# Routing steps go first in a planned instruction list, and gates enter it earlier: attention followed by a sticky mixture of experts on one core

## The chip, the cores and the metric

The kernel runs on one NeuronCore of a Trainium2 chip. The core has a matrix engine (PE, with its weight loads shown as PEld), a vector engine (DVE), an activation engine (ACT), a general engine (POOL) and a queue engine (SP) that here only issues DMAs. Each engine works through its own instructions in order. The metric is device microseconds of one launch, from the first to the last instruction and the little that lies around them.

## The reference

Two stages. First causal attention with a decay, for 8 batches, 8 heads, 576 positions, 64 wide:

```python
scores = scale * np.matmul(q, k.transpose(0, 1, 3, 2))
log_f = np.log(np.clip(f, 0.0001, 1.0))
cum = np.cumsum(log_f, axis=-1)
decay = cum[:, :, :, None] - cum[:, :, None, :]
scores = np.where(causal, -1000000000.0, scores + decay)
attn = softmax(scores)            # max taken off, 1e-9 in the divisor
x = matmul(attn, v)               # (8, 576, 512) after the heads are joined
```

Then each of the 4608 tokens goes through one of 8 experts. The expert is sticky: a token takes the argmax of its own logits where the local gate is below one half (and at position 0), and else the expert of the token before it in its batch.

```python
for b in range(B):
    prev_e = -1
    for s in range(S):
        fresh_e = int(np.argmax(logits[b, s]))
        if s == 0 or local_gate[b, s] < 0.5:
            e = fresh_e
        else:
            e = prev_e if prev_e >= 0 else fresh_e
        prev_e = e
        p = softmax(logits[b, s])
        h = np.maximum(x[b, s] @ w1[e], 0.0)      # 512 -> 1024
        out[b, s] = p[e] * (h @ w2[e])            # 1024 -> 512
```

## The kernel before, in words

**Attention.** Eight batches, one after the other. A batch is cut into 25 units of work (`compute`, from line 836); a unit is a block of 128 queries by up to 512 keys, and passes through stages on different engines: scores on PE (`sc`, L870), row maximum on DVE (`mx`, L881), exponential on ACT (`ex`, L901), transposition of the probabilities on PE (`tr`, L916), their high half on ACT (`hi`, L921), their low half on DVE (`lo`, L925) or, in four units, on PE and ACT (`sub`, `lo2`), products with v on PE (`av`, L895), and the normalisation on DVE (`n1`, `n2`, L956 and L960). Each number in single precision is carried as a high and a low half in 16 bits.

**The list.** Nothing is scheduled at run time. While the program is written, `issue` (L1214) keeps a clock for each engine and, for each stage, the unit that is next in it. It estimates when each could start (`start_of`, L1144), adds that stage's weight `W`, and writes out the instruction whose sum is least; `RANK` decides ties. The costs are constants in the code. Limited buffers (PSUM banks `psS`, `psT`, `psX`, and others) are counted in `room`. `step` (L1253) puts a unit into the lists and issues until that unit's scores are out, so "step 14" of a batch means the place in the list where unit 14 enters.

**What else goes into the list.** While batch b is computed, the next batch's q, k and v are split into halves on POOL, through `queue`, from which `pump` (L310) writes out a share at each step. q and k are then transposed on PE in five groups each (`tq`, L451) and moved out of PSUM by ACT (L460) or DVE (L462, L464) (`eq`). From which step on each group may enter is in `TS`; which engine takes it out (A for ACT, D for DVE) is in `TE`. A finished batch's x is split on POOL (`xr`, and `xl` for its last 64 rows), transposed by DMAs of the SP queue (L756, L785) and written to `xs` in DRAM.

**Gate and routing.** These are the side steps: a chain of small functions, `chain`, of which only the first can go. At step `GI[...]` of batch b, the gate of batch b-1 is put at the front of the chain: `mult` on PE (L819), `half` on ACT, `add` on DVE. In batches 2, 4 and 6 the routing of the two batches before it (a group: 0, 1, 2) is put behind it (`route`, L1333): argmax, the sticky scan, each token's place within its expert, and the inversion of that by matmuls (L1485, L1535). It begins with `mxs` (L1346) and ends with `pinvert2` (L1539). Groups 0 and 1 do part of it on POOL; group 2 does all of that on DVE. Behind group 2 stand `early_idx` and `early_tok`: the indices and the gather (L1628) of 384 tokens of expert 0, which the experts' first matmuls need. `early_tok` may go only once batch 7 has passed step 5, when memory is freed for it. A function that has `yield` in it is several pieces, each with the cost that it yields; `POOL` there means 1500 ns on POOL.

What is left of the chain when attention's lists are empty is written out in order (L1753):

```python
    while chain:
        side_issue(*side_next())
```

**Experts.** Then come the experts (`experts`, L1633): z = x w1 (L1660), relu on ACT (L1646) with its low half on DVE (L1647), y = h w2 (L1674), scaled by ACT (L1651) and scattered by POOL (L1652). Expert 0's first 384 tokens go first; the gate of batch 7 and the last routing group (3) are woven into them.

In what follows a stretch of the trace between attention's last product (L895) and the experts' first (L1660) is called the hole.

Of the kernel before, what the change touches and what calls it, by code (L numbers as in the profile page):

```python
# [38 lines left out]
ORDA = moves_of("q0:P k:M 0:V 1:V k:ag")  # L39
ORDB = moves_of("q:ag q0:T 2:V q1:P k0:P k1:P q:e k:e 3:V q1:T q:Tl k0:T :vl :Vl q:2 q:C 0:K k1:T :iv v0:P k:2 1:K")  # L40

GI = (21, 20, 20)
LI = (14, 18)
PX = 6
XI = 3

TS = {"q": (10, 14, 14, 17, 18), "k": (18, 20, 21, 21, 21)}
TE = {"q": "DDADD", "k": "DDDDA"}

UO = tuple(range(25))  # L50
NP = 0
# [15 lines left out]
def kernel(  # L67
# [13 lines left out]
    B, H, S, D = q.shape  # L81
# [660 lines left out]
        clock["DVE"] += 600  # L742


    XT = {}

    def finish_main(b, xn):
        xr = pools["small"].tile([128, 4, 2, DM], F16, name="xr", bufs=1)
        xt = pools["small"].tile([128, 4, 8, 128], F16, name="xt", bufs=1)
        XT[b] = [xt]  # L750
        xm = xn.rearrange("p (c h) x -> p c (h x)", c=4)
        t0 = b * S
        todo = []

        def turn_x(c):
            nc.sync.dma_start_transpose(out=xt[:, c:c + 2].rearrange("p c a x -> p (c a) x"),  # L756
                                        in_=xr[:, c:c + 2].rearrange("p c a e -> p (c a e)"))
            R[c] = True

        def put_x(r):  # L760
            nc.sync.dma_start(out=xs[t0:t0 + 512].rearrange("(c p r) e -> r p c e", c=4, r=2)[r],
                              in_=xr[r * 64:(r + 1) * 64].rearrange("p c a e -> p c (a e)"))

        R = {}
        bulk.extend([(0 if b == B - 1 else PX + 2 * r, lambda: 2 in R, lambda r=r: put_x(r)) for r in range(2)])
        if b == B - 1:
            def part(c, n, fast, turn):
                split(xr[:, c:c + n, 0, :], xr[:, c:c + n, 1, :], xm[:, c:c + n], fast)
                if turn:
                    turn_x(turn - 1)  # L770

            return [lambda: part(0, 2, False, 1), lambda: part(2, 1, False, 0), lambda: part(3, 1, True, 3)]
        for c in range(0, 4, 2):
            todo += hi_lo(xr[:, c:c + 2, 0, :], xr[:, c:c + 2, 1, :], xm[:, c:c + 2], 1)
            todo.append((0, lambda c=c: turn_x(c)))
        queue.extendleft(reversed(todo))

    def finish_last(b, xnl):
# [5 lines left out]
        def turn_x():  # L784
            nc.sync.dma_start_transpose(out=xlt, in_=xl.rearrange("p a j d -> p (a j d)"))  # L785
            put_xl()

        def put_xl():
            for r in range(2):
# [11 lines left out]
    def gate(b):  # L801
# [29 lines left out]

        if b == B - 1:
            return [lambda: mult((0, 1)), lambda: mult((2, 3, 4)), half, add]
        return [mult, half, add]

    def compute(b, T):
# [293 lines left out]
    STAGES = ("sc", "mx", "mn", "ex", "tr", "hi", "lo", "sub", "lo2", "av", "n1", "n2", "tq", "eq")  # L1130
    RANK = {st: 0.0 for st in STAGES + ("side",)}
    RANK["side"] = -20
    RANK.update({'sc': -20.2, 'mx': 39.7, 'mn': -7.5, 'ex': 80.9, 'tr': -11.9, 'hi': -3.6, 'lo': 1.1, 'sub': 15.5, 'lo2': 1.2, 'av': 12.4, 'n1': -23.3, 'n2': -3.6, 'side': -52.7, 'tq': 30.8, 'eq': -17.3})
    W = {st: 0 for st in RANK}
    W.update({'sc': -100, 'mx': -220, 'mn': -450, 'ex': 40, 'tr': -160, 'hi': -90, 'lo': -350, 'sub': -140, 'lo2': -70, 'av': -70, 'n1': -250, 'n2': -290, 'side': -180, 'tq': -170, 'eq': -430})
    clock = {"PE": T0, "ACT": T0, "DVE": T0, "POOL": T0}
    due = deque()
    pools = {}
# [5 lines left out]
    def start_of(st):  # L1144
# [17 lines left out]
        for r, c in takes.items():  # L1162
            if len(room[r]) < c:
# [4 lines left out]

    COSTS = {"mult": ("PE", 1100), "half": ("ACT", 116), "add": ("DVE", 200), "rows": ("PE", 200), "rows2": ("ACT", 260),
             "ends": ("PE", 30), "carries": ("PE", 30), "back": ("PE", 60), "place": ("PE", 90), "marks": ("DVE", 485),  # L1170
             "prob2": ("ACT", 150), "pmarks": ("DVE", 1500 if B < 2 else 0), "invert": ("PE", 400), "pinvert": ("PE", 600),
             "nop": ("PE", 0), "fill": ("PE", 30)}
    POOL = 1
    OPENS = "mult", "rows", "ends", "carries", "back", "place", "invert", "pinvert", "fill"
    SHUTS = "add", "rows2", "hold", "scan1", "onehot", "place2", "invert2", "pinvert2", "fill2"
    chain = deque()
# [7 lines left out]
    def side_next():  # L1184
        eng, cost = COSTS.get(chain[0].__name__, ("DVE", 160))
        after = [side["end"]]
        if chain[0] is early_tok and "open" not in EX:
            return None, eng, cost
        if chain[0].__name__ in OPENS and side["run"] is None:
            if not room["psS"]:  # L1190
                return None, eng, cost
            after.append(min(room["psS"]))
        return max([clock[eng]] + [t + WAIT[src, eng] for t, src in after]), eng, side["cost"] or cost

    def side_issue(t, eng, cost):
        fn = chain[0]
# [17 lines left out]
    def issue(until=None):  # L1214
        while any(line.values()):
            ready = [(start_of(st), line[st][0][0] + RANK[st], st) for st in STAGES if line[st]]
            if chain:
                ready.append((side_next()[0], serial[0] + RANK["side"], "side"))
            t, _, st = min((x for x in ready if x[0] is not None), key=lambda x: (x[0] + W[x[2]], x[1]))
            if due and due[0][0] <= t and all(room[r] for r in due[0][2]):  # L1220
                due.popleft()[1]()
# [111 lines left out]
    def route(g, last):  # L1333
# [6 lines left out]
        NV = nc.vector  # L1340
# [122 lines left out]
        def marks():  # L1463
# [2 lines left out]
            LO = R["LO"] = rtile([128, GC, 128], F16, "LO")  # L1466
            NV.tensor_tensor(HI, imain.unsqueeze(1).broadcast_to([128, GC, NM]),
                              R["hm"].unsqueeze(2).broadcast_to([128, GC, NM]), ALU.is_equal)
            yield 1400
            if big is NV:  # L1470
                NV.tensor_scalar(RH[:, :, 0], HI, irow[:, 0:1], None, ALU.mult)
                yield 200
                NV.tensor_scalar(RH[:, 4::5, 0], HI[:, 4::5], irow[:, 1:2], None, ALU.mult)
                yield 1900
            else:
                big.tensor_scalar(RH[:, :, 0], HI, irow[:, 0:1], 1.0, ALU.mult, ALU.mult)
                big.tensor_scalar(RH[:, 4::5, 0], HI[:, 4::5], irow[:, 1:2], 1.0, ALU.mult, ALU.mult)
# [48 lines left out]
        def pmarks():  # L1526
            rp = R["rp"] = rtile([128, GC, 3, NM], F16, "rp")
            for j in range(3):
                big.tensor_tensor(rp[:, :, j], R["HI"], pp[:, gs, j].unsqueeze(2).broadcast_to([128, GC, NM]),
                                  ALU.mult)  # L1530

# [170 lines left out]
    EX = {}  # L1702
# [340 lines left out]
```

## Time and profile before

| | us |
|---|---|
| median of 3 runs | 953.27 (949.66 to 957.69) |
| profiled execution | 954.87 |
| its span | 953.2 |
| PE busy in the span | 813.7 (85%) |
| DVE busy | 545.8 (57%) |
| ACT busy | 403.5 (42%) |
| POOL busy | 416.9 (44%) |
| mean granted TensorE clock | 0.939 |

The page gives the busy time of each engine, strips of 40 equal slices in tenths, the chain of work that ended last, and groups of instructions by line. Answers of the trace give the same by stage, and the instructions in order of time: start in us from the span's start, length, engine, line, operation, written from read, count, and in brackets the idle time before and what ended it. An instruction marked SPq or POOLq is one of an engine's queue. Columns of the other views are named where they are shown.

### The profile page before, as it was taken

What the parts mean: (1) busy time and instruction counts of PE and PEld (TensorE: products, weight loads), DVE (VectorE), ACT (ScalarE), POOL (GpSimd) and SP (SyncE); (2) the same over time, 40 slices, a digit from 0 to 9 for tenths busy, and PEclk for the clock granted to TensorE, in tenths of its full rate; (3) what the DMA queues carried; (4) which work ended last, traced back from release to release, by engine and by line L of the source; (5) the groups of instructions that cost most, each with busy time, mean ns of one, the idle gap of its engine ahead of it and who ended that gap; (6) DMA issues with size and microseconds to landing.
All of it is one profiled execution on the core that took longest, in us unless ns stands there. A gap on an engine that the chain in (4) does not pass through costs nothing. (4 is left out here: it accounts for less than half of the span.)

```text
span 953.2 us, 21059 instructions
## 1 busy us (share of the span) xinstructions
PE 813.7 (85%) x8558; PEld 557.8 (59%) x8558; DVE 545.8 (57%) x1135; ACT 403.5 (42%) x769; POOL 416.9 (44%) x479
## 2 busy tenths in 40 slices
PE   4887989999999999711486997799999999999993
PEld 2665878788787878501243663464747465655651
DVE  8775888989988988635272585531425242432200
ACT  4864767777777778500031321221222323131110
POOL 9585975667594946772112304303030212223020
PEclk9888999999999999955698999799999999999997
DMA  6879877697876726150237629927283836423010
GB/s 162 185 149 212 203 153 173 123 209 117 206 146 159 125 58 179 57 138 1 66 117 191 190 89 221 283 58 210 94 231 104 210 128 166 144 78 96 1 41 6
DMA packets 210244, 130.58 MB, mean 137 GB/s; under 512 B 149054, under 2 KB 185024, under 8 KB 210060
## 3 DMA queue, kind: packets, MB, share of 16 engines
q1 hardware_dynamic: 202369, 104.83, 48.3%
q0 software_dynamic: 7776, 24.39, 7.9%
q8 instruction: 68, 1.11, 0.5%
q14 instruction: 31, 0.25, 0.1%
HBM read 77.39 MB, written 20.41 MB: 103 GB/s over the span
## 5 line engine op out<-in xcount | busy, mean ns | idle before, releaser
L1660 PE MATMUL z<-xT,wh 128*128 128x320 f16 (+3 forms) x1088 | 195.2, 299 | 27.8 <-DVE hl L1647 16.4
L901 ACT ACTIVATE P<-st,nm 128x512 f32<-128x512 f32 (+3 forms) x288 | 150.3, 588 | 35.1 <-DVE nm L881 26.1
L1660 PEld LDWEIGHTS <-wh 128*128 128x128 f16 x1088 | 106.2, 99 | 71.6 <-issue 29.5
L881 DVE TENSOR_REDUCE nm<-st 128x1 f32<-128x512 f32 (+4 forms) x264 | 133.1, 542 | 20.2 <-PE st L877 14.3
L1628 POOL DMA_INDIRECT xg<-xs,mg x37 | 44.8, 1212 | 218.5 <-DMA xT<-xg 177.3
L921 ACT CAST ph<-pt 128x512 f16<-128x512 f32 (+1 forms) x200 | 114.1, 584 | 52.2 <-PE pt L916 46.0
L1674 PE MATMUL y<-uh,hh 128*128 128x512 f16 x328 | 125.0, 381 | 7.1 <-ACT o L1651 7.1
L916 PE MATMUL pt<-ident,P 128*128 128x128 f32 x784 | 121.3, 283 | 10.4 <-DVE pl L925 5.8
L925 DVE TENSOR_TENSOR pl<-pt,ph 128x512 f16<-128x512 f32 x168 | 111.0, 674 | 28.6 <-ACT ph L921 20.5
L1646 ACT ACTIVATE hh<-z 128x640 f16<-128x640 f32 (+3 forms) x80 | 48.5, 607 | 184.1 <-PE z L1660 171.2
L1674 PE MATMUL y<-ul,hh 128*128 128x512 f16 x328 | 124.9, 381 | 0.0
L1674 PE MATMUL y<-uh,hl 128*128 128x512 f16 x328 | 124.8, 381 | 0.0
L1660 PE MATMUL z<-xT,wl 128*128 128x320 f16 (+3 forms) x544 | 124.4, 299 | 0.0
L1647 DVE SCALAR_TENSOR_TENSOR hl<-z,hh 128x640 f16<-128x640 f32 (+3 forms) x80 | 55.8, 701 | 114.3 <-ACT hh L1646 114.3
L1674 PEld LDWEIGHTS <-hh 128*128 128x128 f16 x656 | 64.2, 98 | 82.6 <-issue 8.5
L916 PEld LDWEIGHTS pt<-ident,P 128*128 128x128 f32 x784 | 84.7, 143 | 24.3 <-DVE pl L925 7.8
L895 PE MATMUL xp<-VH,ph 128*128 128x65 f16 (+1 forms) x960 | 90.3, 197 | 0.0
L895 PE MATMUL xp<-VL,ph 128*128 128x65 f16 (+1 forms) x960 | 89.1, 195 | 0.0
L895 PE MATMUL xp<-VH,pl 128*128 128x65 f16 (+1 forms) x960 | 88.5, 194 | 0.2
L870 PE MATMUL st<-KB,QB 70*128 70x256 f16 (+4 forms) x448 | 79.5, 288 | 9.8 <-DMA KB<-Ak 6.4
L1652 POOL DMA_INDIRECT out_dram<-o,ms x37 | 39.9, 1077 | 107.8 <-ACT o L1651 66.4
L895 PEld LDWEIGHTS <-ph 128*128 128x128 f16 (+1 forms) x1920 | 80.9, 102 | 9.1 <-issue 5.3
(346 smaller groups left out, 1286.5 us busy)
## 6 DMA issues: line engine op xcount, KB each, us to landing
stg<-in_moe_w_dram SPq DMA_DIRECT2D x64, 512.0 KB
xs<-xr SPq DMA_DIRECT2D x16, 512.0 KB
ldq<-in_q_dram SPq DMA_DIRECT2D x14, 512.0 KB
ldk<-in_k_dram SPq DMA_DIRECT2D x14, 512.0 KB
ldv<-in_v_dram SPq DMA_DIRECT2D x28, 256.0 KB
KB<-Ak SPq DMA_DIRECT2D x14, 256.0 KB
QB<-Aq SPq DMA_DIRECT2D x13, 256.0 KB
ldv<-in_v_dram SPq DMA_DIRECT2D x20, 64.0 KB
```

The source lines that it names most:

```text
L870: nc.tensor.matmul(st[p0:p0 + m, co:co + n], lhsT=queries(lq, kk, h, c), rhs=rhs, start=(ps == 0 and first and co == col), stop=(ps == 1), ...
L881: nc.vector.tensor_reduce(dst, src, axis=AX.X, op=ALU.max, negate=True)
L895: nc.tensor.matmul(xo, lhsT=a[:, c0:c0 + m], rhs=w[:, vi, :], start=False, stop=(i == n - 1 and jj == 2), skip_group_check=True)
L901: nc.scalar.activation(P[:, c0:c1].rearrange("p (k x r) -> p k r x", r=2, x=64), st[:, c0:c1].rearrange("p (k r x) -> p k r x", r=2, x=64) ...
L916: nc.tensor.matmul(U["pt"][:, i * 128:(i + 1) * 128], lhsT=P[:, i * 128:(i + 1) * 128], rhs=ident, is_transpose=True, start=(i == 0), stop ...
L921: nc.scalar.copy(U["ph"][:, :cols], U["pt"][:, :cols])
L925: nc.vector.tensor_tensor(U["pl"][:, :cols], U["pt"][:, :cols], U["ph"][:, :cols], ALU.subtract)
L1628: nc.gpsimd.indirect_dma_start(out=xg, out_offset=None, in_=xs[0:rows], in_offset=bass.IndirectOffsetOnAxis(ap=cols(i), axis=0))
L1646: nc.scalar.activation(hv, z[:, 0:nh, 0:wd], AF.Relu)
L1647: nc.vector.scalar_tensor_tensor(lv, z[:, 0:nh, 0:wd], 0.0, hv, ALU.max, ALU.subtract)
L1660: nc.tensor.matmul(z[:, a, 0:wd], lhsT=w[:, d, fc * 128:(fc + 1) * 128], rhs=xT[:, x, a * wd:(a + 1) * wd], start=(i == 0), stop=(i == len ...
L1674: nc.tensor.matmul(y, lhsT=a[:, fc, t * 128:(t + 1) * 128], rhs=u[:, fc], start=(i == 0), stop=(i == len(prods) - 1))
```

## The change

Numbers and a few lines of the list's writer. `GI`: in batches 2 to 5 the gate enters at step 14, in batches 6 and 7 at step 12, each at 20 before; batch 1 keeps 21. The side steps had one constant weight, -180; now it is set anew before each choice by `side_weight`: -700 if the piece is one of POOL's or can start no later than its engine is free, and 0 if the engine would have to idle for it. The start of a POOL piece is no longer taken from DVE's clock. A gate (but that of batch 7) may go only when all three transposes of its batch's x have been issued, which `XD` counts; until then nothing of the chain goes. The pieces of `marks` and `pmarks` are given other costs, and `pmarks` is cut into pieces. All weights and ranks of the other stages are set anew, and so are `TS` and `TE`: q's groups become ready at later steps, and of the ten groups of a batch ACT takes five instead of two.

```diff
-GI = (21, 20, 20)
+GI = (21, 14, 12)
+
+SW = (-700, 0, 0)
...
-TS = {"q": (10, 14, 14, 17, 18), "k": (18, 20, 21, 21, 21)}
-TE = {"q": "DDADD", "k": "DDDDA"}
+TS = {"q": (13, 17, 18, 19, 20), "k": (19, 20, 20, 21, 21)}
+TE = {"q": "ADDDA", "k": "DAAAD"}
...
-    XT = {}
+    XT, XD = {}, {}
...
             R[c] = True
+            XD[b] = XD.get(b, 0) + 1
...
             put_xl()
+            XD[b] = XD.get(b, 0) + 1
...
+        mult.batch = b
         return [mult, half, add]
...
-    W.update({'sc': -100, 'mx': -220, 'mn': -450, 'ex': 40, 'tr': -160, 'hi': -90, 'lo': -350, 'sub': -140, 'lo2': -70, 'av': -70, 'n1': -250, 'n2': -290, 'side': -180, 'tq': -170, 'eq': -430})
+    W.update({'sc': -210, 'mx': -60, 'mn': -710, 'ex': -30, 'tr': -180, 'hi': -210, 'lo': -140, 'sub': -410, 'lo2': -360, 'av': -130, 'n1': -200,
+              'n2': -170, 'tq': -210, 'eq': -50})
...
-             "prob2": ("ACT", 150), "pmarks": ("DVE", 1500 if B < 2 else 0), "invert": ("PE", 400), "pinvert": ("PE", 600),
+             "prob2": ("ACT", 150), "pmarks": ("DVE", 0), "invert": ("PE", 400), "pinvert": ("PE", 600),
...
-        if chain[0] is early_tok and "open" not in EX:
+        if chain[0] is early_tok and "open" not in EX or XD.get(getattr(chain[0], "batch", None), 0) < 3 and hasattr(chain[0], "batch"):
             return None, eng, cost
...
-        return max([clock[eng]] + [t + WAIT[src, eng] for t, src in after]), eng, side["cost"] or cost
+        now = 0 if side["cost"] is POOL else clock[eng]
+        return max([now] + [t + WAIT[src, eng] for t, src in after]), eng, side["cost"] or cost
+
+    def side_weight(t, eng, cost):
+
+        if t is None:
+            return 0
+        return SW[0] if cost is POOL or t <= clock[eng] + SW[2] else SW[1]
...
                 ready.append((side_next()[0], serial[0] + RANK["side"], "side"))
+                W["side"] = side_weight(*side_next())
...
             for j in range(3):
+                yield 570 if big is NV else POOL
                 big.tensor_tensor(rp[:, :, j], R["HI"], pp[:, gs, j].unsqueeze(2).broadcast_to([128, GC, NM]),
                                   ALU.mult)
```

More of the change, by code (lines that the diff above doesn't have):

```diff
@@ L1132 @@
     RANK["side"] = -20
-    RANK.update({'sc': -20.2, 'mx': 39.7, 'mn': -7.5, 'ex': 80.9, 'tr': -11.9, 'hi': -3.6, 'lo': 1.1, 'sub': 15.5, 'lo2': 1.2, 'av': 12.4, 'n1': -23.3, 'n2': -3.6, 'side': -52.7, 'tq': 30.8, 'eq': -17.3})
+    RANK.update({'sc': 24.3, 'mx': 16.8, 'mn': -67.5, 'ex': 93.3, 'tr': -65.0, 'hi': 26.5, 'lo': -10.3, 'sub': 17.2, 'lo2': 31.3, 'av': 16.7, 'n1': 33.1,
+                 'n2': 10.6, 'side': -52.7, 'tq': 28.8, 'eq': -19.5})
     W = {st: 0 for st in RANK}
-    W.update({'sc': -100, 'mx': -220, 'mn': -450, 'ex': 40, 'tr': -160, 'hi': -90, 'lo': -350, 'sub': -140, 'lo2': -70, 'av': -70, 'n1': -250, 'n2': -290, 'side': -180, 'tq': -170, 'eq': -430})
+    W.update({'sc': -210, 'mx': -60, 'mn': -710, 'ex': -30, 'tr': -180, 'hi': -210, 'lo': -140, 'sub': -410, 'lo2': -360, 'av': -130, 'n1': -200,
+              'n2': -170, 'tq': -210, 'eq': -50})
     clock = {"PE": T0, "ACT": T0, "DVE": T0, "POOL": T0}
@@ L1468, in marks @@
                               R["hm"].unsqueeze(2).broadcast_to([128, GC, NM]), ALU.is_equal)
-            yield 1400
+            yield 320 if big is NV else 1480
             if big is NV:
                 NV.tensor_scalar(RH[:, :, 0], HI, irow[:, 0:1], None, ALU.mult)
-                yield 200
+                yield 250
                 NV.tensor_scalar(RH[:, 4::5, 0], HI[:, 4::5], irow[:, 1:2], None, ALU.mult)
-                yield 1900
+                yield 2060
             else:
```

## The prediction

> **What bounds the kernel now.** I read the utilisation strips of the page first, then the table of busy time by stage, then the order of instructions of PE and of DVE around the hole that the strips show. The strips (40 slices of 23.8 us):
>
> ```profile
> PE   4887989999999999711486997799999999999993
> POOL 9585975667594946772112304303030212223020
> ```
>
> PE is nine tenths busy in attention and again in the experts, and falls to one tenth for two slices between them. The table by stage (stretch, length, then busy time of PE, PEld, DVE, ACT, POOL with counts, granted clock, DMA share, GB/s):
>
> ```profile
> 100.00:406.30 306.30, 290.55 (x4855) 238.24 (x4851) 266.58 (x603) 230.00 (x487) 213.57 (x245) 0.99 0.68 146
> 406.30:438.40 32.10, 3.53 (x30) 2.21 (x28) 10.53 (x33) 1.04 (x3) 24.35 (x34) 0.55 0.39 102
> 438.40:455.90 17.50, 3.87 (x31) 2.31 (x31) 13.14 (x55) 0.63 (x2) 0.00 (x0) 0.50 0.01 1
> 455.90:467.00 11.10, 0.01 (x1) 0.04 (x2) 1.15 (x10) 0.00 (x0) 3.13 (x3) 0.50 0.62 142
> ```
>
> Attention is bound by PE (290.6 of 306.3 us, clock 0.99), with DVE next (266.6). Then come three stretches, 60.7 us together, in which PE does 7.4 us. What fills them is in the order of instructions (start, length, engine, line; first PE's, then DVE's, then POOL's):
>
> ```profile
> 406.05 0.20 PE L895 MATMUL xp<-VH,pl 128*64 128x65 f16 x2
> 426.10 0.22 PE L1442 MATMUL st<-EX,ones 128*128 128x80 f16 x1 [10.04 <-POOL EX L1435]
> 466.99 0.80 PE L1660 MATMUL z<-xT,wh 128*128 128x384 f16 x2 [11.24 <-DMA xT<-xg]
> ```
> ```profile
> 166.25 0.24 DVE L1346 TENSOR_REDUCE mx<-L 128x10 f32<-128x80 f32 x1
> 398.45 0.28 DVE L1539 TENSOR_TENSOR invp<-st,invp 128x120 f32<-128x120 f32 x1 [1.64 <-PE st L1535]
> 398.64 0.23 DVE L1346 TENSOR_REDUCE mx<-L 128x10 f32<-128x80 f32 x1
> 438.58 0.23 DVE L1346 TENSOR_REDUCE mx<-L 128x10 f32<-128x80 f32 x1
> 455.69 0.28 DVE L1539 TENSOR_TENSOR invp<-st,invp 128x120 f32<-128x120 f32 x1 [1.09 <-PE st L1535]
> ```
> ```profile
> 423.09 2.26 POOL L308 TENSOR_TENSOR ul<-stg,uh 128x512 f16<-128x512 f32 x2
> 456.79 1.23 POOL L1628 DMA_INDIRECT xg<-xs,xg  x1 [19.66 <-DVE xe L1569]
> ```
>
> L1346 opens a routing group, the L1539 before the next one closes it. Group 0 runs 166 to 398, spread over five batches. Groups 1 and 2 run after attention with nothing beside them: 40 us and 17 us. Only then can the gather of the early expert's tokens start (456.8) and the first expert matmul (467.0). So the hole is routing that the list pushed out of attention.
>
> **The change, part by part.** *Routing first (weight -700 where the engine need not idle), gates at step 14 or 12.* The question is whether groups 0 to 2 now fit into attention. Step 20's diagonal masks date the steps:
>
> ```profile
> L976 PE MATMUL st<-mB,mA x4: 193/193/202, 341.4 to 341.5; 128*128 128x64 f16 x4
> L976 PE MATMUL st<-mB,mA x4: 193/193/202, 384.8 to 384.9; 128*128 128x64 f16 x4
> ```
>
> A batch is 43.4 us, a step 1.74 us. Group 2 joins the chain at step 12 of batch 6, 8 steps before 341.4: at 327.5. The two costliest DVE groups of attention (busy, mean ns, idle before):
>
> ```profile
> L881 DVE TENSOR_REDUCE nm<-st 128x1 f32<-128x512 f32 (+4 forms) x218 | 109.8, 544 | 5.6 <-PE st L877 3.5 <-PE st L870 1.0
> L925 DVE TENSOR_TENSOR pl<-pt,ph 128x512 f16<-128x512 f32 (+1 forms) x139 | 91.7, 673 | 20.6 <-ACT ph L921 13.9 <-PE xp L895 3.5 <-ACT P L992 1.7
> ```
>
> After a routing piece on DVE the next is not ready at once, so one attention operation (about 0.6 us) goes between, then the piece (about 0.2): 0.8 us a piece. By the code, group 2 has some 52 DVE pieces (42 us), 4 us in its large marks, and some 19 crossings between engines, estimated at 0.6 us: about 57 us. It has 327.5 to 406, 78 us, less the time that the chain stands behind a gate (some 5 us in each of batches 6 and 7) and two gates of 2 us: 64 us. It just fits. Groups 0 and 1, with 17 POOL pieces counted at 1.5 us and four empty steps, come to about 70 us and have two batches each. I take it that all three fit and that the gather (10.2 us from 456.8 to 467.0) lies beside the end of attention, leaving 2 us exposed. Gain: the 60.7 us less what attention grows by.
>
> *What attention grows by.* (a) PE takes in the routing matmuls of groups 1 and 2: 3.5 + 3.9 us at half clock, above; **6 us** (4 to 7.4), as PE has nothing to spare. (b) DVE takes in 10.5 + 13.1 us, about 21 without attention's own tail, and small operations are longer there (min/median/max):
>
> ```profile
> L1397 DVE TENSOR_TENSOR_SCAN crow<-hold,ends x4: 169/626/1115, 223.4 to 483.4; 1x10 f16<-1x10 f32 x4
> L1467 DVE TENSOR_TENSOR HI<-imain,hm x4: 574/576/1339, 317.3 to 491.9; 128x400 f16<-128x400 f16 x4
> L1359 DVE TENSOR_REDUCE F<-eq x4: 227/236/237, 192.4 to 478.1; 128x10 f32<-128x80 f32 x4
> ```
>
> Two-input L1397 and L1467 cost 0.9 and 0.8 us more at 223 and 317, with POOL busy, than alone; the reduction does not. I allow 6 us more for each group. The Trainium skill's page "GPSIMD Engine Reference", section "Key points", says that GpSimd shares its SBUF interfaces with VectorE and collides with DVE instructions that have two SBUF inputs or run in a two-port mode; it speaks against this change, as it puts group 2 beside a working POOL, and the rows agree. By that rule alone DVE would take in 33 us, without it 21.
>
> *Evictions of q's and k's groups.* Three full groups a batch move from DVE to ACT:
>
> ```profile
> L464 DVE COPY Ak<-st x24: 680/692/693, 119.1 to 344.8; 128x1024 f16<-128x1024 f16 x24
> L460 ACT ACTIVATE Aq<-st x6: 1024/1025/1025, 99.1 to 326.5; 128x1024 f16<-128x1024 f16 x6
> ```
>
> Over six batches DVE loses 18 x 0.69 = 12.4 us and ACT gains 18 x 1.02 = 18.4 us, which its 76 idle us cover (306.3 - 230.0). If that cover failed, it would cost at most the 6 us of difference. DVE's net gain in work is 9 to 21 us against 40 idle; the part in batches 6 and 7 comes thick, so **5 us** on the path (-5 to 12). The later steps for q's groups crowd the transposes into steps 17 to 20; I put them, the new ranks and the other weights at nothing (-5 to 8), since PE's own work is unchanged.
>
> (c) *Waits for POOL.* The plan counts 1.5 us for a POOL piece from the end of the one before; in its queue it stands behind all that was pumped. Rows for hand-overs in group 0:
>
> ```profile
> 309.20 1.00 DVE L1459 SCALAR_TENSOR_TENSOR ov<-code,ov 128x10 f32<-128x10 f32 x1
> 340.70 0.23 DVE L1504 TENSOR_REDUCE den<-ex 128x10 f32<-128x80 f32 x1
> ```
> ```profile
> 314.62 0.21 POOL L1461 TENSOR_TENSOR hm<-t,ov 128x10 f16<-128x10 f32 x1
> 341.07 0.40 POOL L1506 TENSOR_TENSOR ex<-ex,OHA 128x80 f32<-128x80 f32 x1 [2.59 <-DVE den L1504]
> ```
>
> One was 4.4 us late, the other 0.1. Before, the slow chain hid it; now the next DVE or PE piece of the routing is queued right behind, and with it all attention work of that engine. Groups 0 and 1 have four such hand-overs each (L1357, L1435, L1461, L1506). The plan covers 1.5 us of it; with one in four 4.4 - 1.5 = 2.9 us late, 8 x 0.25 x 2.9 is **6 us** (0 to 8 x 4.4 = 35).
>
> (d) *Gates ahead of their data.* The guard holds the gate until its three transposes are issued, not until they land. Batch 7:
>
> ```profile
> 371.05 1.05 POOL L1604 TENSOR_SCALAR stg<-stg 128x1024 f32<-128x1024 f32 x1 [7.25 <-DMA stg<-in_moe_w_dram]
> 384.21 0.41 POOL L304 TENSOR_SCALAR xl<-xnl 128x256 f16<-128x256 f32 x1
> 385.40 1.23 SPq L785 DMA_TRANSPOSE xlt<-xl  x1
> 386.04 0.95 PE L819 MATMUL st<-wg,xt 128*128 128x18 f16 x32
> 387.89 0.42 PE L819 MATMUL st<-wg,xlt 128*64 128x18 f16 x8 [0.90 <-DMA xlt<-xl]
> ```
>
> At step 20 PE already waits 0.9 us for xlt. POOL makes xl behind 13 us of weight pieces that start when the first staged block lands (371.1); the list has them by about step 15 (estimated from 17 steps for 24 pieces), so the guard opens there, 5 steps or 8.7 us of PE's time earlier, while POOL gets there no sooner. PE is in order: all of attention stands behind this gate. I take 6 us here and 2 in batches 5 and 6 together: **8 us** (0 to 14).
>
> *The experts' start.* The first 14 matmuls of z against 14 later ones, in the chain of waits:
>
> ```profile
> 466.99 4.45 PE z L1660 x14
> 479.19 2.45 PE z L1660 x14
> 495.59 1.31 PE y L1674 x6
> ```
>
> Without the hole they run at full clock: 2 us saved. The Trainium skill's page "TensorE: Matmul & The Clock Gate", section "Part 1", says that an idle window of about 3.4 us halves the clock. The rows agree for the long hole; by that rule a 6 us stand at (d) would cost some 2 us more, and the sum would be 920. Next to be late would be y, which needs the last weights: POOL ends them at 425.4, 19 us after attention's end, and y comes 28.6 us after z's start. That covers it.
>
> **Sum.** Attention grows by 6 + 5 + 6 + 8 = 25 us and ends at 431.3; z starts at 433.3. Saved: 467.0 - 433.3 + 2 = 35.7. The profiled execution took 954.87 (span 953.2 and 1.7 around it), 1.6 above the median 953.27: 919.2 on its own scale, 918 on the median's.
>
> **Rivals.**
> - *No stall* (chance 0.18): (b), (c) and (d) hide in DVE's 40 and PE's 16 idle us. For it: ACT's slack and 12.4 us off DVE. z at 406.3 + 6 + 2 = 414.3, saved 54.7: about 899.
> - *Routing doesn't get through* (0.20): chain pieces take 1.1 us instead of 0.8, or the gate of batch 6 holds the chain longer, and much of group 2 runs behind attention. For it: only 7 us are spare above. Up to 17.1 + 11.3 us (438.6 to 455.7 to 467.0) stay exposed: attention +16, z at 450.9, saved 16 us: about 938; with the gather alone exposed, 928.
> - *POOL's backlog decides* (0.06, slower): if each of the eight hand-overs of (c) waits 10 us, all of it lands on DVE and PE: 80 us against 41.7 of gain (35.7 + 6), about 992. It decides from 41.7 / 8 = 5.2 us a hand-over. Against it: the longest here is 4.4.
> - *The list shifts the holes about* (0.04): what is saved comes back as bubbles in attention, within 1%.
>
> The forecast itself gets 0.52. The range from 896 to 942 reaches from the no-stall case to the routing rival. A measurement of this kernel can tell about 1% from no change. Faster by over 1% (below 943.7): 0.87; within 1%: 0.07; slower: 0.06.
>
> **What would show it.** Right: L1539 three times before attention's last L895; the gather (L1628) issued before it; z within some 5 us of it; PE's strip without the slices of one tenth; L895 ending near 431. PE waiting at L819 for xlt in batch 7 shows (d), DVE or PE waiting for POOL at L1359, L1442, L1467 or L1510 shows (c). Wrong: an L1346 after the last L895, or attention ending beyond 445.

## Result and the profile after

The changed kernel takes 921.78 us, the median of four runs (920.49 to 926.55). The kernel before took 954.7 us beside it (949.66 to 957.69). The ratio is 0.967, with an interval of 0.961 to 0.973. The profiled execution of the changed kernel took 921.67 us; its span is 919.9 and its granted clock 0.964, where the one before had 953.2 and 0.939.

The first view is again the page's strips of the changed kernel, PE and its clock, in 40 slices, now of 23.0 us.

```profile
PE   5787999889997998688896997899999999999993
PEclk9888999999999999889998998999999999999997
```

The two slices of one tenth are gone. In their place PE's strip has some slices of six to eight tenths inside attention, which stood at nine before. In this version lines 895, 1660, 1628, 1539 and 1346 of before are 900, 1676, 1644, 1555 and 1361. Attention's last product and the experts' first one, from the lists of each line's instructions (min/median/max in ns, first and last start):

```profile
L900 PE MATMUL xp<-VH,pl x960: 190/193/247, 26.0 to 437.0; 128*128 128x65 f16 x128, 128*64 128x65 f16 x64
L1676 PE MATMUL z<-xT,wh x1088: 216/299/421, 437.1 to 898.5; 128*128 128x320 f16 x149, 128*128 128x384 f16 x11, 128*128 128x256 f16 x11, 128*128 128x128 f16 x11
```

Before, these times were 406.1 and 467.0. Attention ends 31 us later, and the experts follow it at once. The order of DVE's and of POOL's instructions shows the three groups and the gather:

```profile
227.30 0.27 DVE L1555 TENSOR_TENSOR invp<-st,invp 128x120 f32<-128x120 f32 x1
253.60 0.22 DVE L1361 TENSOR_REDUCE mx<-L 128x10 f32<-128x80 f32 x1
328.70 0.27 DVE L1555 TENSOR_TENSOR invp<-st,invp 128x120 f32<-128x120 f32 x1
355.27 0.22 DVE L1361 TENSOR_REDUCE mx<-L 128x10 f32<-128x80 f32 x1
414.10 0.28 DVE L1555 TENSOR_TENSOR invp<-st,invp 128x120 f32<-128x120 f32 x1 [0.51 <-PE st L1551]
```
```profile
418.25 1.23 POOL L1644 DMA_INDIRECT xg<-xs,xg  x1 [1.87 <-DVE rs L961]
```

Group 2 is closed at 414.1, and the gather starts at 418.3, 19 us before attention's end.

Where did the 31 us of attention come from? The table by stage, cut at step 20 of batches 1 to 7, at the last product, and with the same columns as the table by stage in the prediction (stretch, length, busy time of PE, PEld, DVE, ACT, POOL with counts, granted clock, DMA share, GB/s). The three stretches shown are the ones that grew, with the sum of all seven. First the kernel before, then the changed kernel.

```profile
162.70:204.30 41.60, 40.76 (x686) 33.95 (x682) 37.63 (x89) 32.83 (x71) 28.31 (x27) 1.00 0.74 151
250.50:293.10 42.60, 41.52 (x710) 34.81 (x704) 38.58 (x90) 33.68 (x73) 33.68 (x35) 1.00 0.77 161
341.40:384.80 43.40, 41.70 (x680) 33.39 (x677) 35.90 (x86) 33.40 (x72) 24.16 (x30) 1.00 0.46 125
sum 292.40, PE 276.67 PEld 226.71 DVE 253.69 ACT 217.85 POOL 200.17; mean PE 39.52 PEld 32.39 DVE 36.24 ACT 31.12 POOL 28.60
```
```profile
157.70:212.00 54.30, 47.69 (x762) 38.48 (x755) 46.44 (x111) 38.42 (x80) 39.94 (x51) 0.97 0.69 151
259.30:313.40 54.10, 46.55 (x761) 37.55 (x754) 45.63 (x110) 38.43 (x80) 39.67 (x50) 1.00 0.65 132
361.10:417.50 56.40, 47.05 (x715) 37.34 (x713) 51.72 (x127) 36.33 (x76) 29.42 (x27) 0.91 0.44 110
sum 325.20, PE 291.32 PEld 236.39 DVE 272.71 ACT 237.25 POOL 216.78; mean PE 41.62 PEld 33.77 DVE 38.96 ACT 33.89 POOL 30.97
```

The stretches shown hold most of a routing group each: group 0 in 157.7 to 212.0, group 1 in 259.3 to 313.4, group 2 in 361.1 to 417.5. They grew by 12.7, 11.5 and 13.0 us. The four stretches left out changed by -3.1, 1.1, -0.6 and -1.8. By the two sum rows the seven stretches grew by 32.8 us, of which PE is busy for 14.6 more (291.3 against 276.7) and idle for 18.2 more (33.9 against 15.7). The grown stretches show that the price is paid where the routing runs, not after it.

PE's waits in the changed kernel, from 112.0 to 437.2 (us in total, times, longest):

```profile
PE pt L921 <- DVE pl L930: 8.3, 11, 1.7
PE st L875 <- ACT P L906: 7.4, 8, 4.6
PE st L823 <- DMA xlt<-xl: 3.7, 2, 2.3
PE xp L900 <- DVE pl L930: 3.5, 4, 1.3
PE pt L921 <- DVE rs L961: 3.0, 4, 1.5
PE st L875 <- DMA KB<-Ak: 1.7, 1, 1.7
PE xp L890 <- DVE xn L965: 1.6, 2, 1.0
```

And in the kernel before, from 113.9 to 406.3:

```profile
PE pt L916 <- DVE pl L925: 5.1, 9, 1.2
PE xp L885 <- DVE xn L960: 2.7, 5, 1.1
PE pt L916 <- ACT P L901: 2.0, 3, 0.9
PE st L1535 <- POOL rp L1529: 1.8, 1, 1.8
PE st L819 <- DMA xlt<-xl: 0.9, 1, 0.9
```

After, 23.8 us of the rows shown are waits for DVE, or for an ACT exponential, which in its turn often waits for DVE's maximum (25.9 us of ACT's time in this stretch of the trace); before, those were 9.8. With the rows under 1 us, which are left out here, it is 25.7 against 11.6: 14.1 us of the 18.2 by which PE is longer idle. The longest of these waits is worth seeing in full, since it shows how group 2's marks are placed. DVE's order in batch 7 of the changed kernel, where ... leaves out two marks:

```profile
380.59 0.65 DVE L1476 TENSOR_TENSOR hm<-t,ov 128x10 f16<-128x10 f32 x1
381.27 1.37 DVE L1482 TENSOR_TENSOR HI<-imain,hm 128x400 f16<-128x400 f16 x1
382.68 1.10 DVE L1486 TENSOR_SCALAR RH<-HI,irow 128x400 f16<-128x400 f16 x1
...
385.23 1.48 DVE L1494 TENSOR_TENSOR LO<-i,lo 128x1280 f16<-128x1280 f16 x1
386.64 0.68 DVE L886 TENSOR_REDUCE nm<-st 128x1 f32<-128x512 f32 x1
```

Six pieces of routing stand in a row, 6.0 us from 380.6 to 386.6, and the maximum that attention waits for comes behind them. The exponential that it releases starts on ACT at 387.35, after ACT had waited 7.0 us for DVE. The next two views are matmuls in PE's order with the waits before them, and PE by stretches of five microseconds (stretch, length, PE's busy time, clock, DMA share, GB/s). PE stands 4.6 us, and the clock is halved in the stretch in which it starts again. A second, shorter loss of clock follows from 401:

```profile
388.11 0.59 PE L875 MATMUL st<-Ak,Aq 128*128 128x512 f16 x1 [4.59 <-ACT P L906]
400.01 0.66 PE L921 MATMUL pt<-ident,P 128*128 128x128 f32 x4 [0.99 <-DVE pl L930]
402.48 1.06 PE L921 MATMUL pt<-ident,P 128*128 128x128 f32 x4 [0.89 <-DVE rs L961]
```
```profile
386.00:391.00 5.00, 2.89 (x11) 0.50 1.09 205
401.00:406.00 5.00, 3.98 (x51) 0.66 0.46 150
```

The Trainium skill's page "TensorE: Matmul & The Clock Gate", section "Part 1", says that one idle window of about 3.4 us brings the half clock. The wait of 4.6 us agrees with that; the trace as a whole does not, as shorter waits were followed by the half clock too. By stretches of one microsecond the clock is 0.50 from 403 to 405, behind waits of 0.99 and 0.89 us, and from 188 to 190, behind one of 1.74 us; in the 4.6 us wait itself, which begins at 383.5, it is 0.73 from 385 to 386 and 0.50 from 386 on. A wait of 1.26 us before 173.1 left it at 1.00. So here some waits of one to two microseconds cost clock and others did not.

### The profile page after: what moved, and what is told of

Read it like the earlier page. It is cut to its first block, busy times and chain, and to the rows that moved or that the text cites. A ratio compares the mean times of both kernels' runs of the same rounds, so it can differ in the third digit from the quotient of the medians.

```text
span 919.9 us, 21034 instructions
## 1 busy us (share of the span) xinstructions
PE 816.4 (89%) x8558; PEld 559.8 (61%) x8558; DVE 538.4 (59%) x1117; ACT 420.4 (46%) x787; POOL 420.9 (46%) x479
## 4 chain that ended last, share of the span: by engine, by line
PE 59%; POOL 13%; DVE 9%; DMA 8%; issue 5%; ACT 3%; SPq 1%; POOLq 0%; ACTq 0%; DVEq 0%
PE z L1676 21%; PE y L1690 18%; PE pt L921 6%; PE st L875 6%; PE xp L900 4%; POOL t16q L310 2%; DMA stg<-in_moe_w_dram 2%; POOL xr L310 2%; DMA out_dram<-o,xs 2%; POOL t16k L310 2%; DMA KB<-Ak 2%; DVE pl L930 1%; ACT P L906 1%; PE st L453 1%; DVE nm L886 1%
## 5 line engine op out<-in xcount | busy, mean ns | idle before, releaser
L1676 PE MATMUL z<-xT,wh 128*128 128x320 f16 (+3 forms) x1088 | 191.6, 296 | 15.4 <-DVE hl L1663 15.2
L906 ACT ACTIVATE P<-st,nm 128x512 f32<-128x512 f32 (+3 forms) x288 | 152.7, 585 | 38.3 <-DVE nm L886 35.4
L926 ACT CAST ph<-pt 128x512 f16<-128x512 f32 (+1 forms) x200 | 116.0, 583 | 62.8 <-PE pt L921 61.5
L921 PE MATMUL pt<-ident,P 128*128 128x128 f32 x784 | 125.6, 284 | 16.8 <-DVE pl L930 9.6
L1644 POOL DMA_INDIRECT xg<-xs,mg x37 | 46.7, 1262 | 188.7 <-DMA xT<-xg 168.3
L900 PE MATMUL xp<-VH,pl 128*128 128x65 f16 (+1 forms) x960 | 92.1, 195 | 4.6 <-DVE pl L930 4.6
L900 PE MATMUL xp<-VH,ph 128*128 128x65 f16 (+1 forms) x960 | 94.1, 198 | 0.9 <-ACT ph L926 0.9
L900 PE MATMUL xp<-VL,ph 128*128 128x65 f16 (+1 forms) x960 | 92.9, 196 | 0.0
L900 PEld LDWEIGHTS <-ph 128*128 128x128 f16 (+1 forms) x1920 | 84.7, 103 | 8.6 <-issue 3.3
```

The lines of the kernel that those rows point to most:

```text
L900: nc.tensor.matmul(xo, lhsT=a[:, c0:c0 + m], rhs=w[:, vi, :], start=False, stop=(i == n - 1 and jj == 2), skip_group_check=True)
L906: nc.scalar.activation(P[:, c0:c1].rearrange("p (k x r) -> p k r x", r=2, x=64), st[:, c0:c1].rearrange("p (k r x) -> p k r x", r=2, x=64) ...
L921: nc.tensor.matmul(U["pt"][:, i * 128:(i + 1) * 128], lhsT=P[:, i * 128:(i + 1) * 128], rhs=ident, is_transpose=True, start=(i == 0), stop ...
L926: nc.scalar.copy(U["ph"][:, :cols], U["pt"][:, :cols])
L1676: nc.tensor.matmul(z[:, a, 0:wd], lhsT=w[:, d, fc * 128:(fc + 1) * 128], rhs=xT[:, x, a * wd:(a + 1) * wd], start=(i == 0), stop=(i == len ...
```

## Experiments

All ratios are against the kernel before, timed on the same chip, with their 95% intervals. The changed kernel itself has 0.967. "Ends" is the start of the last product of attention in the experiment's profile, "z" that of the experts' first matmul; the changed kernel has 437.0 and 437.1.

**The old weights, ranks and evictions, with everything else of the change.**

```diff
-TS = {"q": (13, 17, 18, 19, 20), "k": (19, 20, 20, 21, 21)}
-TE = {"q": "ADDDA", "k": "DAAAD"}
+TS = {"q": (10, 14, 14, 17, 18), "k": (18, 20, 21, 21, 21)}
+TE = {"q": "DDADD", "k": "DDDDA"}
...
(RANK and W of the stages: the numbers of before)
```

> The side steps' new weight, the guard, the early gates and the new piece costs alone; weights and ranks of the other stages and the steps and engines of q's and k's groups as before. Theory A (routing itself makes attention longer, by DVE, PE and POOL work and waits): the hole is gone and attention grows about as in the changed kernel or a little more, since DVE keeps 12.4 us of evictions; 920 to 932. Rival B (the new weights and the crowded transposes make it longer): hole gone without the growth, 895 to 908.

Measured: 936.7 us, ratio 0.980 (0.976 to 0.983). Attention ends at 443.6, z starts at 443.8. The rule for the side steps, with the early gates and the pieces' costs, closes the hole without the new numbers of the stages, at a price of 37.5 us in attention (443.6 against 406.1). The new numbers take 6.6 us off that, and by the ratios some 12 us off the whole time (0.980 against 0.967); 4.9 us of it lie behind z's start (487.7 us of span here, 482.8 in the changed kernel). The time lies above the range that was expected; I had those numbers at nothing.

**The new weights alone: old gates, old constant weight of the side steps.** The pieces' costs, the count of transposes and the start of POOL pieces stay as changed, here and in the other kernels with the old constant weight.

```diff
-GI = (21, 14, 12)
+GI = (21, 20, 20)
-SW = (-700, 0, 0)
+SW = (-180, -180, 0)
```

> The new weights, ranks, steps and engines alone; the side steps keep the constant -180 and the gates step 20. Theory A: the hole stays, attention as before or slightly shorter: 945 to 956. Rival B: the hole stays and attention is 25 to 31 us longer: 975 to 985.

Measured: 945.85 us, ratio 0.987 (0.983 to 0.990). Attention ends at 408.6, z starts at 460.4: the hole is still there, 52 us long. That the new numbers lengthen attention is thereby refuted: it ends only 2.5 us later than before, although it now has most of group 1 beside it, which begins at 327 and is closed at 432, where before it ran from 398.6 to 438.4. The gains of these two kernels, 1.3% and 2.0%, add up to the 3.3% of the whole change.

**The gates back at step 20.**

```diff
-GI = (21, 14, 12)
+GI = (21, 20, 20)
```

> The changed kernel with the gates at step 20 again. In its list group 2 ends nine DVE instructions before attention does, so the gather of the early tokens no longer lies beside attention. Theory A: 5 to 10 us of the gather come out behind attention, 925 to 932. Rival D (early gates cost more by PE waiting for xlt than they bring): some 4 us of waits go, 914 to 920.

Measured: 928.66 us, ratio 0.970 (0.967 to 0.973). Attention ends at 424.9, 12 us sooner than with the early gates, and z starts at 435.1: the gather lies bare, as expected. The order of POOL's instructions in this kernel:

```profile
423.55 1.22 POOL L1644 DMA_INDIRECT xg<-xs,xg  x1 [0.52 <-DVE xe L1585]
```

The shorter attention was not expected. The two stretches in which groups 0 and 1 begin take 48.7 us each here, 54.3 and 54.1 in the changed kernel. So early gates are needed for group 2 and cost something in the batches of groups 0 and 1.

**The old constant weight, with the early gates.**

```diff
-SW = (-700, 0, 0)
+SW = (-180, -180, 0)
```

> The changed kernel with the constant weight -180 for the side steps, gates at 14 and 12 kept. Theory A: group 0 takes as long as before, most of group 1's end and all of group 2 run behind attention, and the hole is back at 35 to 60 us: 940 to 956. Rival E (the early gates alone bring the routing through): 918 to 930.

Measured: 934.27 us, ratio 0.976 (0.974 to 0.979). Attention ends at 411.0 and z starts at 446.2. Groups 0 and 1 get through (closed at 281.2 and 401.3), group 2 runs from 402.1 to 435.0, most of it behind attention. The time lies between the two ranges expected. With the kernel of old gates (hole 52 us), this shows what each part does: the early gates by themselves bring two groups into attention and shorten the hole from 52 to 35 us; the weight of -700 brings in the third. By the kernel with the gates at 20 it does so without early gates too, only too late for the gather.

**The small pieces of groups 0 and 1 on DVE, so that nothing waits for POOL at a hand-over.**

```diff
-        aux, AUX = (nc.gpsimd, POOL) if big is nc.gpsimd else (NV, None)
+        aux, AUX = NV, None
```

> The changed kernel, with the small POOL pieces of groups 0 and 1 (eq, EX, cnt, lo, hm, ex, pp, pe) on DVE instead; the large marks stay on POOL. Theory C (DVE and PE waiting for POOL at the hand-overs is what makes attention longer): those waits go, attention 5 to 10 us shorter, ratio to the kernel before 0.957 to 0.963. Theory F (DVE's own time, with routing pieces ahead of attention's low halves and maxima, is what makes it longer): 14 more pieces a group on DVE, attention 5 to 12 us longer, ratio 0.972 to 0.980.

Measured: 929.88 us, ratio 0.970 (0.964 to 0.977). The groups themselves are shorter, 60 and 62.6 us instead of 73.9 and 75.1, but attention ends at 439.7, 2.7 us later. The ratio lies between the two ranges expected. The edit takes away the hand-overs to POOL (term c) and puts 14 more pieces of each group on DVE, so it shows the sum of both: at most a small gain from the first, or one that the second took back. That the first is small is seen in the changed kernel, where DVE waits 2.4 us for POOL in all of attention and PE not at all.

**Group 2's large pieces on POOL as well.**

```diff
-        big = nc.vector if g >= B // 2 - 2 else nc.gpsimd
+        big = nc.vector if g >= B // 2 - 1 else nc.gpsimd
```

> The changed kernel, with group 2 done as groups 0 and 1 are: its small pieces and large marks on POOL. In its list group 2 ends with attention, so the gather of 10 us comes out behind it. Theory F: batch 7 gets some 8 us shorter by DVE's relief, which the gather takes back: ratio 0.965 to 0.973. Theory C: POOL in batch 7 is full of weight pieces, DVE and PE wait behind them at four hand-overs, some 5 us each: ratio 0.985 to 0.998.

Measured: 953.89 us, ratio 0.998 (0.996 to 1.000): the whole gain is gone. This edit brings about what the rival with POOL's backlog says. DVE's and PE's longest waits in this kernel from 361.2 to 437.4, and the stage behind attention:

```profile
DVE pe L1525 <- POOL ex L1521: 10.3, 1, 10.3
PE pt L921 <- DVE rs L961: 9.7, 1, 9.7
```
```profile
437.40:465.80 28.40, 0.37 (x18) 0.27 (x13) 4.80 (x13) 0.40 (x1) 16.80 (x16) 0.59 0.71 163
```

One hand-over made DVE wait 10.3 us and, through it, PE 9.7. The group is closed at 437.2, 0.2 us before the last product. The steps between it and the gather (4.1 us in the changed kernel, 414.1 to 418.3) fall behind attention, and there the list has POOL's weight pieces (13.6 of the 16.8 us of POOL in that stage; the rest is the gather itself) ahead of the gather, which starts at 455.6. z comes at 465.8. Two things thus turn the result: a hand-over behind POOL's queue, and a group that is closed too late for the gather to be written before attention's end.

**The pieces of groups 0 and 1 back at -180, group 2 as changed.**

```diff
+        if getattr(chain[0], "g", 2) in SLOW or chain[0] is nop:
+            return SLOW_W
         return SW[0] if cost is POOL or t <= clock[eng] + SW[2] else SW[1]
...
+SLOW, SLOW_W = (0, 1), -180
```

> The changed kernel, with the pieces of groups 0 and 1 at the weight -180 again; group 2, the gates and the early tokens keep -700. In its list group 1 ends just ahead of group 2's start, and group 2 ends with attention (672 of 670 DVE instructions), so the gather of 10 us is exposed. Theory F with the price on density (a group that goes through in one batch costs some 12 us, one that is spread costs little): attention 10 to 20 us shorter, 10 us given back: ratio 0.955 to 0.967. If a group costs the same however fast it goes: 0.975 to 0.980.

Measured: 941.79 us, ratio 0.985 (0.981 to 0.990). Step 20 of batch 7 comes at 402.9 instead of 417.5, though some of this is work of group 2 that now stands later. Group 2 starts at 370.6, is closed at 433.9, and the last product is at 432.2. The same cliff shows in POOL's order of this kernel:

```profile
439.35 1.04 POOL L1626 TENSOR_SCALAR stg<-stg 128x1024 f32<-128x1024 f32 x1 [7.88 <-DMA stg<-in_moe_w_dram]
...
448.65 1.23 POOL L1650 DMA_INDIRECT xg<-xs,xg  x1 [0.18 <-issue]
```

The gather stands behind weight pieces for 14.7 us after the group was closed, and z starts at 458.8. For part of that POOL itself stands, until a block of weights lands at 439.35. The ratio lies above both ranges expected: the exposed end cost more than the 10 us that I had allowed, and what a slower passage of groups 0 and 1 is worth is seen here only in part.

**The pieces go first even where their engine has to idle for them**, at a weight of -350 instead of -700.

```diff
-SW = (-700, 0, 0)
+SW = (-350, -350, 0)
```

> The changed kernel with -350 for every side piece, also where its engine would idle for it. In its list group 2 ends 90 DVE instructions before attention does instead of 43. If idling for a routing piece costs what it looks like (some 0.1 to 0.2 us on DVE or PE for each of some 180 pieces): attention 10 to 25 us longer, nothing gained at its end, ratio 0.977 to 0.993. Rival: those gaps lie in slack, and a routing that is through sooner changes nothing: 0.964 to 0.970.

Measured: 942.35 us, ratio 0.984 (0.979 to 0.989). Group 2 takes 27.4 us (351.6 to 379.0) instead of 58.8, the gather starts at 406.1, and attention ends at 449.7, 12.7 us later. PE's waits in this kernel's attention:

```profile
PE xp L900 <- DVE pl L930: 12.2, 6, 3.8
PE st L823 <- DMA xlt<-xl: 11.9, 2, 8.1
```

A chain that is through earlier gains nothing, and a gate ahead of its data does cost what term (d) feared: 8.1 us at one gate. In the changed kernel the longest such wait is 2.3 us. Its rule, "only where the engine need not idle", is the likely reason; the run does not show it alone, since the weight itself changed too.

**Early gates for group 2 alone.**

```diff
-GI = (21, 14, 12)
+GI = (21, 20, 12)
```

> The changed kernel with the gates at step 20 in batches 2 to 5 and at 12 only in batches 6 and 7, so that groups 0 and 1 start after their batch's transposes and group 2 still starts early; in its list group 2 ends 45 DVE instructions before attention does. Theory G (what groups 0 and 1 cost depends on where they fall: started at step 14 they meet the crowd of transposes and evictions of steps 17 to 21): batches 3 and 5 take some 49 us, as in the run with all gates at 20, instead of 54, attention ends some 10 us sooner than in the changed kernel and z follows at once: ratio to the kernel before 0.953 to 0.960. If a group costs the same wherever it starts: the changed kernel's ratio, 0.964 to 0.970.

Measured: 919.22 us, ratio 0.961 (0.958 to 0.965), just above the range expected. Attention ends at 424.2, 12.8 us sooner than in the changed kernel, and z follows at 424.4. The stretch of group 0 in this kernel:

```profile
158.10:206.20 48.10, 43.81 (x727) 35.84 (x724) 43.28 (x110) 36.75 (x76) 27.91 (x31) 1.00 0.70 151
```

It takes 48.1 us, and group 1's takes 48.1 us as well, 6 less each than in the changed kernel. Its profiled execution is 9.2 us shorter (span 910.7 against 919.9), as 3.5 us come back behind z; it is the fastest of the six executions, 6.8 us under their median. So where groups 0 and 1 begin in their batch is worth some 12 us of attention in these profiles. This confirms what the kernel with the gates at 20 had suggested.

**The list counts 500 ns for a small piece instead of 160.**

```diff
-        eng, cost = COSTS.get(chain[0].__name__, ("DVE", 160))
+        eng, cost = COSTS.get(chain[0].__name__, ("DVE", 500))
...
-            side["cost"] = next(side["run"]) or 160
+            side["cost"] = next(side["run"]) or 500
```

> The changed kernel with 500 ns instead of 160 as the list's cost of a small routing piece; group 2's pieces took 0.44 us each on DVE beside attention in the changed kernel, and 0.26 behind it in the kernel before. In its list group 2 ends 28 DVE instructions before attention does. Theory H (the list runs away from the chip: it counts 160 for a piece that takes 440, so PE arrives early at what DVE has not done): PE's waits for DVE in batches 3, 5 and 7 shrink and attention ends 8 to 15 us sooner: ratio 0.950 to 0.960. If the waits come from DVE's work itself, whatever the list believes: 0.963 to 0.972.

Measured: 926.7 us, ratio 0.969 (0.965 to 0.972): no gain. Attention ends at 429.4, 7.6 us sooner than in the changed kernel, just short of the 8 to 15 us that theory H expected, but the time behind z grows: 489.9 us of span from z's start, 482.8 in the changed kernel. The loss is in the first 175.6 us after z. There PE does 144.2 us of work here and 151.4 in the changed kernel. These are the rows of this kernel:

```profile
PE z L1676 <- DVE hl L1663: 16.3, 4, 9.0
PE y L1690 <- ACT o L1667: 9.6, 1, 9.6
```

In the changed kernel the same two waits take 13.3 and 6.4 us. What makes the experts' first stage later was not tried.

**The changed kernel again**, with no edit, on the same chip as the last two and beside them.

> The changed kernel once more, beside these two on one chip: every theory expects its ratio of 0.967 again, within 0.961 to 0.973.

Measured: 924.92 us, ratio 0.966 (0.962 to 0.970). Attention ends at 438.1, z starts at 438.3. The figures of the changed kernel hold in this second set of runs, and early gates for group 2 alone have the lower ratio beside it, 0.961 (0.958 to 0.965); the two intervals overlap by a little.

**Early gates for group 2 alone, and its probabilities behind attention.** Of group 2 only what the gather needs stays in attention. Its probabilities, `pinvert` and the fill of the early expert's table come after the last product and ahead of z.

```diff
-GI = (21, 14, 12)
+GI = (21, 20, 12)
...
-        return steps + [fill, fill2] if g == B // 2 - 2 else steps
+        if g == B // 2 - 2:
+            LATE.extend(rest + [pinvert, pinvert2, fill, fill2])
+            return crit + [invert, invert2]
+        return steps
...
+    chain.extend(LATE + [early_probs])
```

> The kernel with only group 2's gate early, and group 2 cut in two: places and indices in attention as there, its probabilities (27 of its DVE pieces, some 11 us of DVE's time beside attention) in order behind attention, before z. Theory F (each microsecond of routing on DVE in batch 7 costs attention about half of one): attention ends 5 to 7 us sooner, at about 418, and the tail behind it takes 8 to 9 us: z at 427, ratio 0.962 to 0.968. If the density of pieces is the price: attention 8 to 13 us shorter, ratio 0.955 to 0.962. If DVE's work is not what costs: attention ends at 424 as there, ratio 0.968 to 0.974.

Measured: 917.0 us, ratio 0.960 (0.958 to 0.962), the lowest of all. Attention ends at 419.7, 4.5 us sooner than with early gates for group 2 alone (424.2). That is a little less than the 5 to 7 us of theory F; the ratio fell in the range of the theory that the density of pieces is the price. From 100 us to the last product DVE has 25 instructions and 7.7 us of work less than in that kernel (272.7 against 280.4 us), not the 11 us that I had reckoned with, and PE 1.1 us less. So a microsecond of DVE taken out here is worth some 0.4 to 0.6 us of attention, as PE's own share is left out or not. What moved behind stands for 12.5 us before z, which starts at 432.2, 7.8 us later than in that kernel; of this the time behind z gives 4.4 us back (481.9 us of span from z's start, 486.3 there). By their intervals the two cannot be told apart in time. Both have a lower ratio than the changed kernel, by 0.5 to 0.7%, with intervals that just overlap with its own.

## Why the prediction was right, and where its terms were off

**What bounds the kernel: right.** The hole of 60.7 us was routing that the list had pushed out: the old constant weight in the changed kernel brings back a hole of 35 us, and with the old gates as well one of 52.

**All three groups fit: right.** Group 2 ran from 355.3 to 414.1, 58.8 us, against 57 worked out (52 pieces at 0.8 and the rest). It joined the chain later than I took it and had room because attention's end moved with it. How near the edge this is was seen better in the runs than in my 7 spare us: two kernels whose group 2 was closed 0.2 us before and 1.7 us after the last product have a hole of 28 and 27 us, not the 10.2 of the gather, since POOL's weights stand in the list at that place. The rival "routing doesn't get through" had this as 10 to 28 us; the cliff is at its upper end.

**The gather beside attention: right.** The 2 us that I left exposed are 0.1.

**The experts' start: right in kind.** The first 14 matmuls of z, from the chain of waits of the changed kernel, against 4.45 us before, and y:

```profile
437.19 2.38 PE z L1676 x14
466.60 1.70 PE y L1690 x6
```

2.07 us saved, 2 predicted; y is 29.4 us behind z's start, 28.6 before, so its cover held.

**Attention's growth: 30.9 us (406.3 to 437.2), 25 predicted.** This is the whole miss: z at 437.1 instead of 433.3, and the time 921.78 instead of 918. By terms, with what was measured:

- (a) PE's routing matmuls, 6 predicted: right. The routing matmuls of groups 1 and 2 took 2.5 us each beside attention, by PE's busy time on their lines. PE's 14.6 us more are mostly that and the clock: 0.91 over 56.4 us, 0.97 over 54.3 and 0.96 over 47.3 (the stretch from 212.0, not shown) are worth 5.1 + 1.6 + 1.9 = 8.6 us by the rows, against 1.5 before. As an estimate that makes 5.1 + 7.1 = 12.2 of the 14.6; some 1.3 us of the lost clock fell on an idle PE, from 385 to 388, so it is rather 11.
- (b) DVE's extra work, 5 predicted: mis-sized, and the one term of the sum that was much too cheap. PE's waits for DVE, directly or by way of ACT, are 14.1 us more, and losses of clock follow some of them. I had set 9 to 21 us of extra work against 40 us of idle time, as if a sum of idle time could take it in. The work comes in runs, like the 6.0 us from 380.6 to 386.6, with attention's maximum behind it; and it is longer there than alone (below). The size of the work was right: DVE's busy time in the seven stretches grew by 19.0 us (272.7 against 253.7). The kernel with the probabilities taken out gives a rate: 0.4 to 0.6 us of attention for a microsecond of DVE.
- (c) Waits for POOL, 6 predicted: too large. The changed kernel's DVE waits 2.4 us for POOL in all, at two of the four places named, and PE none. That POOL's queue can turn the result is shown by group 2 on POOL: there one hand-over of 10.3 us, together with the gather's place in the list, undid the gain, where I had reckoned with eight of 5.2 us.
- (d) Gates ahead of xlt, 8 predicted, 6 of them in batch 7: too large and misplaced. PE waits 3.7 us for xlt (0.9 before), in batches 4 and 6 and not at all in batch 7, where the gate stands at 408.6 with its data there: POOL had split xl at 380.1, ahead of its weight pieces, which start at 393.7. The mechanism exists (8.1 us at one gate in the kernel that idles for its pieces).
- Weights, ranks and evictions, "at nothing": wrong by 6.6 us, to the good. With the old ones attention is 6.6 us longer, which is beyond the -5 that I allowed, and the whole time by the ratios some 12 us.
- Not in the prediction at all: the step at which groups 0 and 1 begin. Early gates there lengthen attention by some 12 us in the profiles for nothing that is needed, as group 2 alone decides when the gather goes. The change as it stands pays for this.

So it is partly luck that the sum came out near: (c), (d) and the weights at nothing were too dear by 4 + 5 + 7 us, and (b) with its clock and the early gates of groups 0 and 1, by difference, too cheap by some 22 (16 and the 5.9 by which attention grew more).

**What stays open.** Why groups 0 and 1 cost less when they begin 6 steps later is not settled; the profile shows fewer waits of PE in those stretches and 12 us less POOL work (27.9 against 39.9), which stands in the next stretch there, and no run separates these. From 100 us to the last product PE is busy for 6.0 us less (297.0 against 302.9) with nearly as many matmuls (4904 and 4917), at a clock of 0.99 instead of 0.97, and idle for 6.7 us less: clock and waits have about half each. Of the 12.8 us that attention gains by it, only some 6 us were seen in the medians of runs beside each other (919.2 against 924.9). Moving small pieces of groups 0 and 1 from POOL to DVE, or group 2's pieces from DVE to POOL, moved attention's end by less than 3 us, so the 18 us of PE's idle time are not split between the two engines by these runs.

## What to carry to other kernels

Work that is moved beside a busy engine should be costed by what stands behind it in that engine's order, run by run, and not by the engine's idle time in sum: 19 us of DVE work in 40 us of idle time still cost PE 14 us of waits and some clock. Ask of each early start which later step needs it: here only the last group fed the gather, and starting the others early cost some 12 us of attention. Where a result must be ready before a list's end, look at what the list writes next on that queue, as two chains that were closed at attention's end had their gather 15 and 18 us later, behind POOL's weights.

## What the runs showed of the hardware

Group 2's small DVE pieces took 0.435 us each beside attention (23.9 us for 55), and 0.266 each alone (14.6 for 55), in the kernel before. The same marks, alone, in DVE's order of the kernel before:

```profile
446.46 0.17 DVE L1461 TENSOR_TENSOR hm<-t,ov 128x10 f16<-128x10 f32 x1
446.73 0.57 DVE L1467 TENSOR_TENSOR HI<-imain,hm 128x400 f16<-128x400 f16 x1
447.34 0.32 DVE L1471 TENSOR_SCALAR RH<-HI,irow 128x400 f16<-128x400 f16 x1
...
448.34 1.49 DVE L1479 TENSOR_TENSOR LO<-i,lo 128x1280 f16<-128x1280 f16 x1
```

POOL's order in the changed kernel at that time shows what differs:

```profile
381.18 1.05 POOL L306 TENSOR_SCALAR xr<-xn 128x1024 f16<-128x1024 f32 x1
382.31 2.48 POOL L310 TENSOR_TENSOR xr<-xn,xr 128x512 f16<-128x512 f32 x2
```

HI went from 0.57 to 1.37 us and RH from 0.32 to 1.10 while POOL worked (381.2 to 384.8). The last mark, LO, begins at 385.2, when POOL is done, and takes its 1.48 us as before. ACT stood idle from 380.3 to 387.3 and PE from 383.5, when a mark of 128x80 (383.8 to 384.8) was still slow, 1.01 us against 0.24 alone; and DMA went on while LO ran (share 0.6 to 0.9 from 385 to 387). That leaves POOL as the cause in these rows. I had expected longer two-input pieces; RH has one tensor input and became three times as long.

The Trainium skill's page "GPSIMD Engine Reference", section "Key points", names DVE instructions in a two-port mode beside those with two SBUF inputs. These rows agree with the two-input part; that RH runs in such a mode is not shown by any row here.
